# A hand-paced first pass becomes a table of single-engine pieces: block attention with two feed-forward layers

## The chip, the cores and the metric

The kernel runs on one core of one Trainium2 chip. The metric is device time in microseconds (us) from launch to end. A profiled execution adds a trace, in which the span runs from the first to the last instruction.

## The reference, cut to what matters

```python
# attention inside chunks of 64 tokens: q, k, v are (4, 8, 576, 64)
scores = q_c @ k_c^T / 8;  attn = exp(scores - max) / (sum + 1e-9);  x = attn @ v_c
# x becomes (2304 tokens, 512)
h = x @ w_in1;  g = s * relu(h)**2 + b;          x = g @ w_out1     # 512 -> 2048 -> 512
h = x @ w_in2;  g = h * tanh(log1p(exp(h)));     out = g @ w_out2   # 512 -> 2048 -> 512
```

All data are float32, and the weights arrive as 64-bit words.

## The kernel before, in words

**Tiles.** The 2304 tokens are 18 attention tiles of 128 tokens, gathered in five blocks of 512, 256, 512, 512 and 512 tokens (tiles 0 to 3, 4 and 5, 6 to 9, 10 to 13, 14 to 17). Each feed-forward layer has 16 columns of 128 hidden units (`f`), worked in four groups of four. So there are eight groups, each with 20 steps (five blocks times four `f`). A step is one `mm_in` (12 matmuls into a bank `hp`), the elementwise work that ends in two operands `ghi` and `glo`, and one `mm_out` (12 matmuls into the four sum banks `acc0` to `acc3`). Matmul operands are split in a high and a low part, so that each product takes three matmuls. Before a weight can be used it is loaded (`load_w`, 512 KB) and decoded: one ACT operation, four on DVE, a copy on ACT (`decode_hi`), and a subtraction on DVE (`decode_lo`). A group has eight such parts.

**Attention of a tile.** TensorE transposes k (`k_pe`, 4 matmuls), ACT copies it out in two halves into a block-diagonal key buffer `kbd` (`k_out`). The same for q (`q_pe`, `q_out`). Then 16 score matmuls (`s_pe`), max and subtraction on DVE (`s_max`), exp on ACT (`s_exp`), sum, reciprocal and scaling (`s_sum`), a transpose of the result (`p_pe`, `p_out`), 32 small matmuls with v (`x_pe`), and a split into high and low part (`x_out`: ACT, then DVE).

**Order.** Each engine works through its instructions in the order in which the program gives them. The first pass (attention, group 0 of layer 1) is ordered by hand under `manual_schedule`. First all early loads are issued (`LOADS`); the v loads of tiles 0 to 3 (`V0` to `V3`, four DMAs each) go through ACT's own DMA queue, all others through SP's. Then the string `START` runs tiles 0 to 3 and the decoding of the first two weight parts. Its `w3` and the like are idle matmuls on zeros. After it, a loop of 17 steps puts one step of group 0 together with pieces of four later tiles: x of tile step+1, p of step+2, scores of step+3, k and q of step+4. One weight part or two are decoded per step where `DECODE` says so. In this loop the attention has two PSUM banks (`ps_t`); `ps_at` gives the first four tiles seven banks in turn. Key buffers are four for the first four tiles, and one (`kbd[0]`) afterwards. After `no_sync_barrier` the last three steps of group 0 and groups 1 to 7 follow, put in order by the framework's scheduler, with the `mm_out` of a step two steps behind its `mm_in`.

Of the kernel before, what the change touches and what calls it, by code (L numbers as in the profile page):

```python
# [15 lines left out]
P = 128  # L16
# [16 lines left out]
def chunk_attention_moe_moe_kernel(  # L33
# [44 lines left out]
    ps_t = ctx.enter_context(tc.tile_pool(name="ps_t", bufs=2, space=bass.MemoryType.PSUM))  # L78
# [31 lines left out]
    def decode_w(l, f, part):  # L110
        decode_a(l, f, part)
        decode_b(l, f, part)

    def decode_a(l, f, part):
        decode_a1(l, f, part)
        decode_a2(l, f, part)

    def decode_a1(l, f, part):
# [18 lines left out]
    def decode_a2(l, f, part):  # L137
# [11 lines left out]
    def decode_b(l, f, part):  # L149
        decode_hi(l, f, part)  # L150
        decode_lo(l, f, part)

    def decode_hi(l, f, part):
# [20 lines left out]
    kbd = {}  # L174
# [53 lines left out]
    def transposes(i, src):  # L228
        p = ps_at(i, [P, KD, P])
# [4 lines left out]
    def k_pe(i):  # L234
        at[i]["kp"] = transposes(i, at[i]["k"].rearrange("p h d -> p (h d)"))

    def k_out(i, alt=False):
        kb = kbd[i if i < NS else 0]
# [5 lines left out]
        at[i]["kb"] = kb

    def q_pe(i):
        at[i]["qp"] = transposes(i, at[i]["q"].rearrange("p h d -> p (h d)"))

    def q_out(i, alt=False):
        at[i]["qt"] = sb_at(i, "qt").rearrange("p (a s) -> p a s", a=KD)  # L250
        eng = nc.vector.tensor_copy if alt else nc.scalar.copy
        eng(out=at[i]["qt"], in_=at[i].pop("qp"))
        if NS <= i and i + 2 < NTILE:
            load_qk(i + 2, "k")
            load_qk(i + 2, "q")

    def s_pe(i):
        t = at[i]
        t["sp"] = ps_at(i, [P, H, CH])
# [50 lines left out]
    def x_out(i, alt=False):  # L310
        xp = at.pop(i)["xp"]
        b, o = home[i]
        hi, lo = xhi[b][:, :, o:o + P], xlo[b][:, :, o:o + P]
        nc.scalar.activation(out=hi, in_=xp, func=AF.Copy)
        nc.vector.tensor_tensor(out=lo, in0=xp, in1=hi.bitcast(F32), op=ALU.subtract)  # L315
        if NS <= i and i + 3 < NTILE:
            load_v(i + 3)


    def mm_in(l, f, b, spare):  # L320

        n = sizes[b]
        pool, tag = (ps_t, "t") if spare and f % 2 else (ps_h, "h")
# [25 lines left out]
    def ew_b(l, r, n):  # L349
        hi = sb.tile([P, TB], F32R, tag="ghi", bufs=3, name="ghi")[:, :n]  # L350
        lo = sb.tile([P, TB], F32R, tag="glo", bufs=3, name="glo")[:, :n]
        if l == 1:
            nc.scalar.activation(out=r, in_=r, func=AF.Identity, bias=b_sb[:, 0:1])  # L353
        nc.scalar.activation(out=hi, in_=r, func=AF.Copy)  # L354
        nc.vector.tensor_tensor(out=lo, in0=r, in1=hi.bitcast(F32), op=ALU.subtract)  # L355
        return hi, lo
# [17 lines left out]

    def add_up(l, grp, b, acc):

        t0, n = blocks[b]
        for m, a in enumerate(acc):
            w = n if l == 1 else DM
            y = ysum[b][:, m * w:(m + 1) * w]  # L380
            if grp == 0:
                if m % 2:
                    nc.vector.tensor_copy(out=y, in_=a[:, :w])
                else:
                    nc.scalar.copy(out=y, in_=a[:, :w])
# [18 lines left out]

    pend = []
    accs = {}

    def out_half(h):
        l, grp, b, f, g = pend[0]
        if h == 0 and f % FG == 0:  # L410
            accs[l, b] = [
                ps_acc.tile([P, TB], F32, tag=f"acc{m}", name=f"acc{m}")
                for m in range(KD if l == 1 else sizes[b] // P)
            ]
        mm_out(l, f, g, accs[l, b], sizes[b], h)
        if h == 1:
            pend.pop(0)
            if f % FG == FG - 1:
                add_up(l, grp % NG, b, accs.pop((l, b)))

    first, second = chunk_parts(0), chunk_parts(1)
    DECODE = {0: first[2:4], 1: first[4:6], 2: first[6:7], 3: first[7:8]}
    DECODE.update(zip((7, 9, 10, 11, 13, 14, 15, 16), ([z] for z in second)))
    with tc.manual_schedule():
        nc.scalar.preload_act_table_set("exp_and_others")
        for w in LOADS.split():
            i = int(w[1:])
            if w[0] == "W":
                load_w(*first[i])
            elif w[0] in "vV":  # L430
                load_v(i, nc.scalar if w[0] == "V" else nc.sync)
            elif w[0] == "s":
                nc.sync.dma_start(out=s_sb, in_=s_in.partition_broadcast(P))
                nc.sync.dma_start(out=b_sb, in_=b_in.partition_broadcast(P))
            else:
                load_qk(i, w[0])
        x_tiles(0)
# [3 lines left out]
        warm = ps_t.tile([P, TB], F32, tag="t", name="warm")  # L441

        def warm_up(n):
            for _ in range(n):
                nc.tensor.matmul(out=warm[:, :P], lhsT=zero, rhs=zero)

        kbd[0] = atp.tile([P, KD, 2, P], F32, name="kbd")
# [131 lines left out]
```

## Time and profile before

| | us |
|---|---|
| median of 3 runs (range) | 922.19 (921.17 to 923.06) |
| profiled execution, its own time | 922.06 |
| its span | 920.3 |
| PE, DVE, ACT busy | 880.0, 480.9, 368.7 |

PE is TensorE's matmuls, PEld its weight loads, DVE VectorE, ACT ScalarE, POOL GpSimd; SPq and ACTq are DMA issues from those queues. PEclk is the granted TensorE clock as a share of 2.4 GHz (0.5 is 1.2 GHz). Matmul ends are modelled, and a row's duration runs a little into the next row; the distance between starts is the safer number. The windows view lists, for each stretch, its length, each engine's busy us with its instructions in brackets, PEclk, the DMA engines' busy share and GB/s. The lines view gives busy us in total, mean ns of one, and the idle time before.

### The profile page before, as it was taken

The page shows a single profiled execution, that of the slowest core. Times are in us where ns is not written, and L with a number is a line of the kernel's source. Part 1 is how long each engine was busy: PE and PEld are TensorE (multiplying, and loading weights), DVE is VectorE, ACT ScalarE, POOL GpSimd, SP SyncE. Part 2 cuts the span into 40 slices and gives each one's busy share as a digit, 9 for nine tenths or more (in the row PEclk, how much of TensorE's full clock was granted, in tenths as well). Part 3 has the DMA queues.
Part 4 walks back from the last instruction along what each step waited for, and adds up shares of the span by engine and source line. Part 5 has one row for each costly group of instructions (what it writes and reads, how often), then busy time and mean ns, then how long its engine had stood idle before and what let it go on. Part 6 is the DMA issues. An engine that isn't in the chain of part 4 may idle for free.

```text
span 920.3 us, 12036 instructions
## 1 busy us (share of the span) xinstructions
PE 880.0 (96%) x4878; PEld 735.8 (80%) x4878; DVE 480.9 (52%) x851; ACT 368.7 (40%) x643; POOL 33.9 (4%) x33
## 2 busy tenths in 40 slices
PE   4878889999999999999999999999999999999998
PEld 4656777778888888888988888888888888888886
DVE  1767667768833694359635971166225932222223
ACT  1555556656543463334544542233222322222221
POOL 1100000000000000000212220000000000000000
PEclk7978999999999999999999999999999999999999
DMA  9524463205000410023001400041003200001012
GB/s 251 149 47 115 121 162 98 46 1 160 24 1 1 124 59 1 1 69 115 1 1 37 125 22 1 5 133 46 0 1 93 90 1 1 0 1 46 24 46 91
DMA packets 81526, 53.20 MB, mean 58 GB/s; under 512 B 58688, under 2 KB 75072, under 8 KB 81472
## 3 DMA queue, kind: packets, MB, share of 16 engines
q1 hardware_dynamic: 77120, 51.39, 19.1%
q10 hardware_dynamic: 4352, 1.05, 0.5%
q8 instruction: 38, 0.62, 0.3%
q14 instruction: 16, 0.13, 0.0%
HBM read 47.71 MB, written 4.72 MB: 57 GB/s over the span
## 4 chain that ended last, share of the span: by engine, by line
PE 82%; DVE 9%; ACT 5%; DMA 2%; issue 1%; POOL 0%; DVEq 0%; ACTq 0%; POOLq 0%
PE hp L331 41%; PE acc L368 39%; DMA v<-in_v_dram 2%; DVE wdec L144 1%; DVE wdec L140 1%; ACT e L281 1%; ACT kbd L243 1%; ACT w L157 1%; DVE sm L286 1%; DVE e L275 1%; DVE xlo L315 1%; DVE mx L274 1%; DVE e L290 1%; DVE w L162 1%; DVE wdec L132 1%
## 5 line engine op out<-in xcount | busy, mean ns | idle before, releaser
L331 PE MATMUL hp<-xhi,w 128*128 128x512 f32 (+1 forms) x1280 | 373.1, 373 | 2.6 <-ACT w L157 1.7
L331 PEld LDWEIGHTS hp<-xhi,w 128*128 128x128 f32 x1280 | 233.3, 190 | 47.1 <-issue 2.7
L331 PE MATMUL hp<-xlo,w 128*128 128x512 f32 (+1 forms) x640 | 237.6, 371 | 0.1
L355 DVE TENSOR_TENSOR glo<-r,ghi 128x512 fp32r<-128x512 f32 (+1 forms) x160 | 104.9, 656 | 215.3 <-ACT ghi L354 214.9
L368 PE MATMUL acc<-ghi,w 128*128 128x512 f32 (+1 forms) x640 | 164.8, 375 | 2.5 <-DVE w L162 1.9
L368 PE MATMUL acc<-w,ghi 128*128 128x512 f32 x576 | 159.6, 390 | 0.0
L346 ACT ACTIVATE r<-hp 128x512 f32<-128x512 f32 (+1 forms) x80 | 44.4, 555 | 255.1 <-PE hp L331 255.1
L331 PEld LDWEIGHTS hp<-xlo,w 128*128 128x128 f32 x640 | 121.6, 190 | 21.6 <-DVE xlo L315 0.8
L368 PEld LDWEIGHTS acc<-ghi,w 128*128 128x128 f32 x640 | 113.7, 190 | 22.1 <-DVE w L162 2.2
L368 PEld LDWEIGHTS acc<-w,ghi 128*128 128x128 f32 x576 | 106.9, 188 | 21.3
L387 DVE TENSOR_TENSOR ysum<-acc,ysum 128x512 f32<-128x512 f32 (+1 forms) x114 | 71.8, 655 | 59.5 <-PE acc L368 59.5
L341 ACT ACTIVATE r<-hp 128x512 f32<-128x512 f32 (+1 forms) x80 | 44.1, 551 | 132.1 <-PE hp L331 132.0
L354 ACT ACTIVATE ghi<-r 128x512 fp32r<-128x512 f32 (+1 forms) x160 | 94.1, 588 | 4.5
L368 PE MATMUL acc<-glo,w 128*128 128x512 f32 (+1 forms) x320 | 94.1, 370 | 0.0
L368 PE MATMUL acc<-w,glo 128*128 128x512 f32 x288 | 93.9, 389 | 0.0
L342 DVE SCALAR_TENSOR_TENSOR r<-r,s_sb 128x512 f32<-128x512 f32 (+1 forms) x80 | 56.4, 705 | 67.3 <-ACT r L341 67.2
L353 ACT ACTIVATE r<-r,b_sb 128x512 f32<-128x512 f32 (+1 forms) x80 | 54.6, 682 | 51.2 <-DVE r L342 51.0
L368 PEld LDWEIGHTS acc<-glo,w 128*128 128x128 f32 x320 | 58.4, 189 | 10.3
L368 PEld LDWEIGHTS acc<-w,glo 128*128 128x128 f32 x288 | 54.1, 188 | 11.3
L157 ACT ACTIVATE w<-wdec 128x512 fp32r<-128x512 f32 x64 | 40.3, 630 | 54.4 <-DVE wdec L144 54.0
L162 DVE TENSOR_TENSOR w<-wdec,w 128x512 fp32r<-128x512 f32 x64 | 44.9, 703 | 2.9 <-ACT w L157 2.0
L140 DVE SCALAR_TENSOR_TENSOR wdec<-wraw,wdec 128x512 uint32<-128x512 uint32 x64 | 44.0, 693 | 0.6
(302 smaller groups left out, 494.7 us busy)
## 6 DMA issues: line engine op xcount, KB each, us to landing
wraw<-in_moe_w_in_dram SPq DMA_DIRECT2D x32, 512.0 KB, 3.9
wraw<-in_moe_w_out_dram SPq DMA_DIRECT2D x32, 512.0 KB, 3.5
out_dram<-ysum SPq DMA_DIRECT2D x18, 256.0 KB, 2.0
k<-in_k_dram SPq DMA_DIRECT2D x16, 256.0 KB, 2.9
v<-in_v_dram SPq DMA_DIRECT2D x56, 64.0 KB, 3.3
q<-in_q_dram SPq DMA_DIRECT2D x12, 256.0 KB, 2.9
v<-in_v_dram ACTq DMA_DIRECT2D x16, 64.0 KB, 4.1
k<-in_q_dram SPq DMA_DIRECT2D x4, 256.0 KB, 4.8
```

The costliest lines, as they stand in the source:

```text
L140: nc.vector.scalar_tensor_tensor(out=u, in0=t[:, :, 1], scalar=0xC0000000, in1=u, op0=ALU.bitwise_and, op1=ALU.bitwise_or,)
L157: nc.scalar.activation(out=w[:, 0], in_=a, func=AF.Copy)
L162: nc.vector.tensor_tensor(out=lo, in0=a, in1=hi.bitcast(F32), op=ALU.subtract)
L331: nc.tensor.matmul(out=hp, lhsT=w[:, sl], rhs=r[b][:, a, :], start=(a == 0 and p == 0), stop=(a == KD - 1 and p == 2),)
L341: nc.scalar.activation(out=r, in_=hp, func=AF.Relu)
L342: nc.vector.scalar_tensor_tensor(out=r, in0=r, scalar=s_sb[:, 0:1], in1=r, op0=ALU.mult, op1=ALU.mult)
L346: nc.scalar.activation(out=r, in_=hp, func=AF.Mish)
L353: nc.scalar.activation(out=r, in_=r, func=AF.Identity, bias=b_sb[:, 0:1])
L354: nc.scalar.activation(out=hi, in_=r, func=AF.Copy)
L355: nc.vector.tensor_tensor(out=lo, in0=r, in1=hi.bitcast(F32), op=ALU.subtract)
L368: nc.tensor.matmul(out=acc[m][:, :n] if l == 1 else acc[m], lhsT=w[wi][:, sl] if l == 1 else g[gi][:, sl], rhs=g[gi] if l == 1 else w[wi], ...
L387: nc.vector.tensor_tensor(out=y, in0=a[:, :w], in1=y, op=ALU.add)
```

## The change

`LOADS`, the loop of 17 steps and `DECODE` go. The whole first pass, with all 20 steps of group 0 and all its loads, becomes one table `START` of 600 pieces, each of which runs on one engine or issues one load. A piece may name its PSUM bank (`@0` to `@3` are the sum banks, `@4` and `@5` the two banks that attention had before) or its key buffer (`.0` to `.2`, three instead of four and one). The letters: `dk dq dv` loads of a tile, `W` load of a weight part, `K Q S T X` the matmuls of k, q, scores, transposed p and x; `k q m e n z t x y` what ACT and DVE do after them (`n` sum and reciprocal, `z` scaling, `x` high and `y` low part); `a c d h l` the steps of decoding; `I J` and `O P` the halves of `mm_in` and `mm_out`; `r u v g o` the elementwise work; `E` the first sums, each copied out alone; `w` idle matmuls. `I5` is step 5.

Tiles start in the order 3, 2, 4, 0, 7, 1, 5, 6, 8 and so on. Only tile 0's v goes through ACT's queue. All scalings run on DVE (three of the first four were on GpSimd), and all copies of k, q and p on ACT (`alt` is gone). Of group 1's eight weight parts five are decoded in the table and three (`parts[13:]`) at the start of group 1. Groups 1 to 7 are unchanged, but now start with no `mm_out` pending.

```diff
-LOADS = "k0 q0 V0 k1 q1 V1 k2 q2 V2 W0 k3 q3 V3 W1 k4 q4 W2 W3 s0 k5 q5 v4 W4 W5 v5 W6 W7 v6"
+
 START = (
...
+    "dk3 dq3 dv0 dv3 K3@4 dk2 dq2 k3.0 w3 Q3@5 dk4 q3 dq4 w9 S3@0 W0 dk0 sb m3 w3 K2@1 dv2 k2.1 w3 Q2@2 e3 w3 "
+    "K4@3 q2 n3 dk7 k4.2 S2@4 W5 z3 Q4@5 dv4 m2 a0 T3@0 q4 t3 w3 K0@1 c0 e2 S4@2 k0.0 W2 d0 X3@3 dk1 dq1 K7@5 n2 "
+    "h0 x3 dq7 m4 a5 W4 k7.1 dk5 y3 e4 dq5 c5 a2 dq0 z2 dv1 d5 w24 K1@4 T2@0 k1.2 Q1@1 n4 h5 w3 Q7@2 q1 c2 W3 t2 "
+    "S1@5 dq9 q7 z4 dv5 d2 X2@3 T4@4 l5 x2 K5@1 h2 S7@0 m1 k5.2 W1 Q0@2 dk6 y2 a4 Q5@5 dk8 q0 m7 q5 dq8 w4 S0@1 "
+    "e1 l2 t4 dv7 S5@3 e7 m0 a3 X4@2 n1 e0 Q9@5 W7 x4 n0 dv6 q9 y4 w15 K6@0 z0 k6.1 m5 w3 T0@4 dk9 K8@1 t0 dq10 "
+    "z1 Q8@5 k8.0 X0@2 dk10 n7 e5 dq13 T1@0 q8 c3 x0 W6 S8@3 t1 n5 X1@4 d3 K9@1 x1 y0 h3 dk13 z7 k9.2 w3 Q10@5 z5 "
+    "dq6 T7@0 q10 K10@2 l3 t7 T5@1 y1 dk14 k10.0 X7@5 l0 W10 a1 c4 I2 W12 a7 dv8 x7 c1 t5 I0 d4 X5@0 d1 W9 h4 J0 "
+    "W11 x5 dv9 c7 h1 J2 y5 r0 l1 S9@4 d7 r2 W13 a6 I3 W14 u2 W15 h7 Q6@2 W8 l4 v2 J3 dq14 l7 q6 g2 y7 I1 a10 u0 "
+    "a12 o2 S6@1 v0 m8 r3 J1 g0 m6 e8 I4 K13@0 o0 J4 e6 dk11 u3 k13.2 Q13@2 K14@5 n6 dq11 r1 v3 m9 dk12 I5 q13 g3 "
+    "J5 k14.1 u1 O0 o3 v1 z6 e9 P0 r4 n8 n9 T6@4 g1 I6 t6 z8 J6 o1 X6@5 z9 r5 u4 O1 u5 x6 dv10 c6 v4 v5 T8@4 y6 "
+    "P1 t8 d6 X8@5 g4 c10 h6 S13@4 x8 dv13 o4 l6 I7 r6 y8 a9 O2 u6 m13 v6 Q11@5 P2 q11 dq12 d10 e13 T9@4 g5 O3 "
+    "n13 t9 h10 o5 X9@5 E0.0 E0.1 S10@4 z13 x9 dv12 l10 P3 y9 a11 m10 Q12@5 g6 I8 E0.2 dq15 E0.3 q12 e10 J7 o6 "
+    "c12 O4 r7 n10 J8 u7 I9 z10 v7 r8 c9 P4 u8 J9 g7 d9 v8 O5 o7 I10 h9 c11 r9 l9 P5 u9 T10@4 a8 O6 d12 g8 v9 "
+    "T13@5 P6 t10 o8 t13 J10 d11 g9 h12 X13@4 o9 r10 h11 X10@5 l12 x13 dv14 u10 O7 x10 y13 I11 v10 E1.1 E1.0 y10 "
+    "dv11 K11@4 l11 P7 k11.2 c8 K12@5 J11 E1.2 E1.3 g10 d8 dk17 k12.0 S11@4 dk16 r11 o10 S12@5 h8 m11 O8 m12 e11 "
+    "Q14@4 P8 q14 dq17 n11 e12 S14@5 u11 n12 O9 v11 m14 g11 K17@4 P9 k17.2 dk15 o11 z11 e14 Q17@5 O10 z12 q17 "
+    "dq16 n14 T11@4 T12@5 l8 t11 P10 z14 t12 T14@4 X11@5 t14 O11 x11 dv17 y11 X14@4 E2.0 E2.1 X12@5 x14 dv16 P11 "
+    "y14 x12 y12 S17@4 E2.2 E2.3 dv15 I12 m17 I13 e17 K15@5 n17 J13 k15.0 z17 Q15@4 r13 K16@5 J12 q15 u13 k16.1 "
+    "S15@4 v13 r12 I14 g13 m15 I15 u12 e15 o13 J14 v12 n15 g12 Q16@5 r14 T17@4 z15 J15 q16 o12 t17 u14 S16@5 r15 "
+    "v14 O12 u15 g14 m16 T15@4 v15 P12 t15 o14 e16 X15@5 g15 n16 O13 x15 o15 z16 X17@4 y15 P13 x17 y17 T16@5 O14 "
+    "t16 X16@4 P14 x16 y16 O15 I16 E3.0 E3.1 P15 J16 E3.2 E3.3 I17 r16 u16 I18 v16 J17 g16 o16 J18 r17 u17 I19 "
+    "r18 v17 u18 O16 g17 v18 J19 o17 g18 P16 o18 r19 u19 O17 v19 g19 P17 o19 O18 P18 O19 E4.0 E4.1 P19 E4.2 E4.3"
 )
...
-    ps_t = ctx.enter_context(tc.tile_pool(name="ps_t", bufs=2, space=bass.MemoryType.PSUM))
+    ps_t = ctx.enter_context(tc.tile_pool(name="ps_t", bufs=1, space=bass.MemoryType.PSUM))
...
+    def ps_at(b, shape):
+
+        if b < KD:
+            return ps_acc.tile(shape, F32, tag=f"acc{b}", name="pa")
+        return ps_t.tile(shape, F32, tag=f"t{b - KD}", name="pt_")
...
-    def k_out(i, alt=False):
-        kb = kbd[i if i < NS else 0]
+    def k_out(i, n):
+        at[i]["kb"] = kb = kbd[n]
...
-            eng = nc.vector.tensor_copy if alt and j else nc.scalar.copy
-            eng(out=kb[sl, :, :, sl], in_=kp[sl])
...
+            nc.scalar.copy(out=kb[sl, :, :, sl], in_=kp[sl])
...
-        eng = nc.gpsimd if i < NS and not alt else nc.vector
-        eng.tensor_tensor(out=e, in0=e, in1=sm.to_broadcast([P, H, CH]), op=ALU.mult)
...
+    def s_norm(i):
+        e = at[i]["e"]
+        nc.vector.tensor_tensor(out=e, in0=e, in1=at[i].pop("sm").to_broadcast([P, H, CH]), op=ALU.mult)
...
+        elif name == "dv":
+            load_v(i, nc.sync if i else nc.scalar)
...
+        rest = parts[13:] if grp == 1 else []
+        for step in range(NB * FG):
             b, f = step // FG, f0 + step % FG
+            for z in rest[2 * step:2 * step + 2]:
+                decode_w(*z)
```

## Rows read from the trace of the kernel before

**Rows 1.** The page, part 2: the span in 40 slices of 23 us.
```profile
PE   4878889999999999999999999999999999999998
PEclk7978999999999999999999999999999999999999
```

**Rows 2.** Windows view: three stretches of the first pass, its end, two later groups.
```profile
0.00:42.10 42.10, 26.34 (x294) 23.45 (x295) 17.98 (x36) 15.37 (x28) 7.39 (x13) 0.84 0.83 219
42.10:126.48 84.38, 69.83 (x594) 57.29 (x594) 55.19 (x103) 45.07 (x83) 0.00 (x0) 0.88 0.40 100
126.48:202.89 76.41, 70.90 (x627) 56.14 (x625) 54.46 (x101) 45.30 (x82) 0.00 (x0) 1.00 0.27 67
202.89:221.00 18.11, 18.11 (x79) 14.67 (x80) 13.29 (x23) 9.46 (x16) 0.00 (x0) 1.00 0.46 136
221.00:319.66 98.66, 98.66 (x482) 83.58 (x481) 58.02 (x102) 48.38 (x82) 0.00 (x0) 1.00 0.13 41
319.66:418.32 98.66, 98.66 (x482) 83.58 (x481) 57.65 (x102) 44.15 (x75) 0.00 (x0) 1.00 0.14 43
```

**Rows 3.** Timeline of the start: start us, us, engine, line, operation, idle before.
```profile
0.76 16.24 ACTq L224 DMA_DIRECT2D v<-in_v_dram  x16
4.63 1.92 PE L231 MATMUL pa<-ident,k 128*128 128x128 f32 x8
17.10 0.58 ACT L243 COPY kbd<-pa 64x512 f32<-64x512 f32 x1 [15.09 <-DMA v<-in_v_dram]
18.55 1.98 PE L263 MATMUL pa<-kbd,v 128*64 128x128 f32 x16 [10.83 <-DVE kbd L243]
20.57 0.69 DVE L274 TENSOR_REDUCE mx<-pa 128x8 f32<-128x512 f32 x1 [1.20 <-PE pa L263]
42.10 1.01 PE L331 MATMUL hp<-xhi,w 128*128 128x512 f32 x2 [1.67 <-ACT w L157]
```

**Rows 4.** Waits view of PE, 42 to 126.5 us: total us, times, longest.
```profile
PE pt__519 L263 <- ACT qt L252: 3.7, 1, 3.7
PE acc L368 <- DVE w L162: 1.9, 1, 1.9
```

**Rows 5.** Timeline of PE: one piece of each kind at full clock.
```profile
142.83 0.60 PE L231 MATMUL pt__1432<-ident,q 128*128 128x128 f32 x4
143.36 1.15 PE L308 MATMUL pt__1445<-e,v 64*64 64x64 f32 x32
176.77 1.09 PE L263 MATMUL pt__1799<-kbd,qt 128*64 128x128 f32 x16
210.12 0.62 PE L331 MATMUL hp<-xhi,w 128*128 128x512 f32 x2
212.84 1.98 PE L368 MATMUL acc<-ghi,w 128*128 128x512 f32 x8
```

**Rows 6.** Lines view by shape, DVE and ACT, 0 to 221 us.
```profile
L144 DVE SCALAR_TENSOR_TENSOR wdec<-wraw,wdec 128x512 uint32<-128x512 uint32 x18 | 12.5, 692 | 0.6
L132 DVE TENSOR_SCALAR wdec<-wdec 128x512 uint32<-128x512 uint32 x18 | 7.7, 427 | 0.6
L288 DVE RECIPROCAL sm<-sm 128x8 f32<-128x8 f32 x18 | 3.7, 203 | 0.6
L342 DVE SCALAR_TENSOR_TENSOR r<-r,s_sb 128x512 f32<-128x512 f32 x15 | 11.2, 747 | 11.3 <-ACT r L341 11.3
L281 ACT ACTIVATE e<-e 128x512 f32<-128x512 f32 x18 | 11.4, 631 | 6.2 <-DVE e L275 6.2
L353 ACT ACTIVATE r<-r,b_sb 128x512 f32<-128x512 f32 x15 | 10.9, 726 | 3.6 <-DVE r L342 3.5
```

**Rows 7.** DMA: rate of the first 35 us in 40 slices, and issues from SP.
```profile
GB/s 0 0 108 283 287 280 278 289 287 287 304 387 315 288 288 341 379 290 286 230 164 131 364 354 327 50 171 289 249 126 86 280 301 205 324 277 220 378 417 320
1.85 0.91 SPq L211 DMA_DIRECT2D k<-in_k_dram  x1
76.85 2.58 SPq L224 DMA_DIRECT2D v<-in_v_dram  x4
```

More of the change, by code (lines that the diff above doesn't have):

```diff
@@ L1 @@
+import re
 from contextlib import ExitStack
@@ L126, in decode_a1, with decode_c @@
             nc.vector.tensor_scalar(
-                out=u, in0=t[:, :, 1], scalar1=0x7FFFFFFF, scalar2=None, op0=ALU.bitwise_and
+                out=a.bitcast(U32), in0=t[:, :, 1], scalar1=0x7FFFFFFF, scalar2=None, op0=ALU.bitwise_and
             )
+    def decode_c(l, f, part):
+        t, a = raw[l, f, part]
+        u = a.bitcast(U32)
         nc.vector.tensor_scalar(
@@ L135, in decode_a1, with decode_d @@
         )
-    def decode_a2(l, f, part):
+    def decode_d(l, f, part):
         t, a = raw[l, f, part]
@@ L147, in decode_a2, with decode_h @@
         )
[L149 to L153, printed above, removed]
+    def decode_h(l, f, part):
         a = raw[l, f, part][1]
@@ L157, in decode_hi, with decode_l @@
         nc.scalar.activation(out=w[:, 0], in_=a, func=AF.Copy)
-    def decode_lo(l, f, part):
+    def decode_l(l, f, part):
         hi, lo = wt[l, f, part]
@@ L162, in decode_lo, with decode_w @@
         nc.vector.tensor_tensor(out=lo, in0=a, in1=hi.bitcast(F32), op=ALU.subtract)
+    def decode_w(*z):
+        for step in (decode_a, decode_c, decode_d, decode_h, decode_l):
+            step(*z)
     def runs(t0, n):
@@ L227, in load_v, with transposes @@
                     )
-    def transposes(i, src):
-        p = ps_at(i, [P, KD, P])
+    def transposes(b, src):
+        p = ps_at(b, [P, KD, P])
         for a in range(KD):
@@ L232, in transposes, with k_pe @@
         return p
[L234 to L238 removed]
+    def k_pe(i, b):
+        at[i]["kp"] = transposes(b, at[i]["k"].rearrange("p h d -> p (h d)"))
+    def k_out(i, n):
+        at[i]["kb"] = kb = kbd[n]
         kp = at[i].pop("kp").rearrange("p a (c s) -> p a c s", c=2)
@@ L241, in k_out, with q_pe, q_out, s_pe @@
             sl = slice(j * CH, (j + 1) * CH)
-            eng = nc.vector.tensor_copy if alt and j else nc.scalar.copy
-            eng(out=kb[sl, :, :, sl], in_=kp[sl])
[L244 to L249, printed above, removed]
-        at[i]["qt"] = sb_at(i, "qt").rearrange("p (a s) -> p a s", a=KD)
[L251 to L257, printed above, removed]
+            nc.scalar.copy(out=kb[sl, :, :, sl], in_=kp[sl])
+    def q_pe(i, b):
+        at[i]["qp"] = transposes(b, at[i]["q"].rearrange("p h d -> p (h d)"))
+    def q_out(i):
+        at[i]["qt"] = sb_at(i, "qt").rearrange("p (a s) -> p a s", a=KD)
+        nc.scalar.copy(out=at[i]["qt"], in_=at[i].pop("qp"))
+    def s_pe(i, b):
         t = at[i]
-        t["sp"] = ps_at(i, [P, H, CH])
+        t["sp"] = ps_at(b, [P, H, CH])
         for a in range(KD):
@@ L347, in ew_a, with ew_u, ew_v, ew_g @@
         return r
-    def ew_b(l, r, n):
+    def ew_u(r):
+        nc.vector.scalar_tensor_tensor(
+            out=r, in0=r, scalar=s_sb[:, 0:1], in1=r, op0=ALU.mult, op1=ALU.mult
+        )
+    def ew_v(r):
+        nc.scalar.activation(out=r, in_=r, func=AF.Identity, bias=b_sb[:, 0:1])
+    def ew_g(r, n):
         hi = sb.tile([P, TB], F32R, tag="ghi", bufs=3, name="ghi")[:, :n]
+        nc.scalar.activation(out=hi, in_=r, func=AF.Copy)
+        return hi
+    def ew_o(r, hi, n):
         lo = sb.tile([P, TB], F32R, tag="glo", bufs=3, name="glo")[:, :n]
+        nc.vector.tensor_tensor(out=lo, in0=r, in1=hi.bitcast(F32), op=ALU.subtract)
+        return lo
+    def ew(l, hp, n):
+        r = ew_r(l, hp, n)
         if l == 1:
[L353 to L356, printed above, removed]
+            ew_u(r)
+            ew_v(r)
+        hi = ew_g(r, n)
+        return hi, ew_o(r, hi, n)
     def mm_out(l, f, g, acc, n, h):
@@ L373, in mm_out, with first_sum @@
             )
+    def first_sum(b, m, a, eng):
+        y_tile(b)
+        n = sizes[b]
+        eng(out=ysum[b][:, m * n:(m + 1) * n], in_=a[:, :n])
     def add_up(l, grp, b, acc):
@@ L381, in add_up @@
             if grp == 0:
[L382 to L385, printed above, removed]
+                (nc.vector.tensor_copy if m % 2 else nc.scalar.copy)(out=y, in_=a[:, :w])
                 continue
@@ L403, in chunk_parts @@
         return sorted(z, key=lambda z: (z[1] + z[2], z[2]))
[L405 to L419, printed above, removed]
@@ L421, in chunk_attention_moe_moe_kernel, with new_accs, pieces @@
-    first, second = chunk_parts(0), chunk_parts(1)
-    DECODE = {0: first[2:4], 1: first[4:6], 2: first[6:7], 3: first[7:8]}
-    DECODE.update(zip((7, 9, 10, 11, 13, 14, 15, 16), ([z] for z in second)))
+    parts = chunk_parts(0) + chunk_parts(1)
+    ff = {}
+    first_acc = {}
+    def new_accs(l, b):
+        return [
+            ps_acc.tile([P, TB], F32, tag=f"acc{m}", name=f"acc{m}")
+            for m in range(KD if l == 1 else sizes[b] // P)
+        ]
+    def pieces(name, i, m, bank):
+        b, f = divmod(i, FG)
+        n = sizes[b] if b < NB else 0
+        if name in ("dk", "dq"):
+            load_qk(i, name[1])
+        elif name == "dv":
+            load_v(i, nc.sync if i else nc.scalar)
+        elif name == "sb":
+            nc.sync.dma_start(out=s_sb, in_=s_in.partition_broadcast(P))
+            nc.sync.dma_start(out=b_sb, in_=b_in.partition_broadcast(P))
+        elif name in "KQSTX":
+            dict(K=k_pe, Q=q_pe, S=s_pe, T=p_pe, X=x_pe)[name](i, bank)
+        elif name == "k":
+            k_out(i, m)
+        elif name in "qmenztxy":
+            dict(q=q_out, m=s_max, e=s_exp, n=s_sum, z=s_norm, t=p_out, x=x_hi, y=x_lo)[name](i)
+        elif name in "Wacdhl":
+            dict(W=load_w, a=decode_a, c=decode_c, d=decode_d, h=decode_h, l=decode_l)[name](*parts[i])
+        elif name == "w":
+            for _ in range(i):
+                nc.tensor.matmul(out=warm[:, :P], lhsT=zero, rhs=zero)
+        elif name == "I":
+            ff[i] = {}
+            ff[i]["h"], ff[i]["half"] = mm_in(1, f, b, False)
+            ff[i]["half"](0)
+        elif name == "J":
+            ff[i]["half"](1)
+        elif name == "r":
+            ff[i]["r"] = ew_r(1, ff[i]["h"], n)
+        elif name == "u":
+            ew_u(ff[i]["r"])
+        elif name == "v":
+            ew_v(ff[i]["r"])
+        elif name == "g":
+            ff[i]["g"] = ew_g(ff[i]["r"], n)
+        elif name == "o":
+            ff[i]["o"] = ew_o(ff[i]["r"], ff[i]["g"], n)
+        elif name in "OP":
+            if name == "O" and f == 0:
+                first_acc[b] = new_accs(1, b)
+            mm_out(1, f, (ff[i]["g"], ff[i]["o"]), first_acc[b], n, "OP".index(name))
+        elif name == "E":
+            first_sum(i, m, first_acc[i][m], nc.vector.tensor_copy if m % 2 else nc.scalar.copy)
+        else:
+            raise ValueError(name)
@@ L424, in chunk_attention_moe_moe_kernel @@
     with tc.manual_schedule():
         nc.scalar.preload_act_table_set("exp_and_others")
[L426 to L436, printed above, removed]
@@ L440, in chunk_attention_moe_moe_kernel @@
         make_identity(nc, ident)
[L441 to L447, printed above, removed]
+        warm = ps_h.tile([P, TB], F32, tag="h", name="warm")
         room = sb.tile([P, 2, KD, 2, P], F32, tag="ysum3", name="kbd12")
-        kbd[1], kbd[2] = room[:, 0], room[:, 1]
-        kbd[3] = sb.tile([P, KD, 2, P], F32, tag="ysum2", name="kbd3")
@@ L451, in chunk_attention_moe_moe_kernel @@
-        for kb in kbd.values():
+        kbd = [atp.tile([P, KD, 2, P], F32, name="kbd"), room[:, 0], room[:, 1]]
+        for kb in kbd:
             nc.gpsimd.memset(kb, 0.0)
-        by_name = dict(w=warm_up, K=k_pe, k=k_out, Q=q_pe, q=q_out, S=s_pe, m=s_max, e=s_exp, n=s_sum,
-                       T=p_pe, t=p_out, X=x_pe, x=x_out,
-                       A=lambda i: decode_a(*first[i]), B=lambda i: decode_b(*first[i]))
         for w in START.split():
-            by_name[w[0]](int(w[1]), *[True] * (w[2:] == "*"))
@@ L524, in chunk_attention_moe_moe_kernel, with do_out @@
-        for z in late:
-            decode_lo(*z)
-    tc.no_sync_barrier()
-    for grp in range(2 * NG):
+            name, i, m, bank = re.fullmatch(r"([a-zA-Z]+)(\d*)(?:\.(\d))?(?:@(\d))?", w).groups()
+            pieces(name, int(i or 0), int(m or 0), int(bank or 0))
+    tc.no_sync_barrier()
+    pend = []
+    accs = {}
+    def do_out():
+        l, grp, b, f, g = pend.pop(0)
+        if f % FG == 0:
+            accs[l, b] = new_accs(l, b)
+        for h in range(2):
+            mm_out(l, f, g, accs[l, b], sizes[b], h)
+        if f % FG == FG - 1:
+            add_up(l, grp % NG, b, accs.pop((l, b)))
@@ L529, in chunk_attention_moe_moe_kernel @@
+    for grp in range(1, 2 * NG):
         l, f0 = chunks[grp * FG]
-        to_load, to_decode = (chunk_parts(grp + 1), chunk_parts(grp + 1)) if grp else ([], [])
-        for step in range(0 if grp else NTILE - 1, NB * FG):
+        to_load, to_decode = chunk_parts(grp + 1), chunk_parts(grp + 1)
+        rest = parts[13:] if grp == 1 else []
+        for step in range(NB * FG):
             b, f = step // FG, f0 + step % FG
+            for z in rest[2 * step:2 * step + 2]:
+                decode_w(*z)
```

140 lines of the change are left out of this document (28 added, 112 removed).

## The prediction

> **What bounds the kernel now.** I read the page first [rows 1]. From its tenth slice on, PE is full at the full clock; all that can be won lies in the first 220 us, and the granted clock is low only there. The windows put borders to it [rows 2]. A later group of 20 steps takes 98.66 us with PE busy for all of it; two in a row agree to the hundredth. So from 221.0 us on, where PE begins group 1, the kernel is bound by PE, and 699.3 of the 920.3 us lie there.
>
> The first pass needs far less PE time than the 221.0 us it takes. A q transpose is 0.60, the scores 1.09, the x matmuls 1.15 us [rows 5]; neighbouring rows overlap by some 0.07, as the q row that starts at 142.83 and the x row at 143.36 show. A tile is three transposes at 0.59, 1.03 and 1.08, which is 3.9 us, and 18 tiles are 70. A half step is 2.72 us (from 210.12 to 212.84 for 12 matmuls), half of that in block 1, and a group is 98. Before 221.0 us PE does all attention and group 0 but two `mm_out`: 70 + 98 - 5.4 = 163 us. So 58 us are lost, and the stretches of [rows 2] say where.
>
> In 0 to 42.1 us, four tiles are 15.5 us of work: 26.6 lost. In 42.1 to 126.5 PE does steps 0 to 7, the `mm_out` of steps 0 to 6, and 8 k, 8 q, 8 scores, 6 p, 6 x: 59 us of work, 25 lost. Of these, 14.5 are idle time (84.4 less 69.8 busy) and the rest is the clock, granted at 0.88. In 126.5 to 202.9 it is 69 us of work, 7 lost; to 221.0 almost nothing.
>
> The reasons differ. At the start, k was transposed at 4.63 us, but ACT copied it out only at 17.10, since it stood in its own queue of 16 v issues for 16.24 us; the first scores came at 18.55 [rows 3]. Later PE waits for whatever the hand order put in its way: 3.7 us for `qt`, which ACT copies late, 1.9 for a decoded weight [rows 4]. No other engine is full: DVE is busy for 55 of 84 us, ACT for 45.
>
> **The change, part by part.** *ACT's queue.* Twelve of 16 v issues move to SP. On ACT they took 16.24 us together [rows 3], so four take about 4. The first k copy can start at some 5 us, the first scores at 7 to 8 and the first max at 9, where it was at 20.57. SP pays instead: 2.58 us for four v issues [rows 7], 7.7 for twelve.
>
> *The loads.* In front of `dk10`, the last load that the PE pieces before `I2` need, the table has 20 k and q, 8 v and 7 W. The first k and q loads ran at some 283 GB/s [rows 7], 0.93 us for 256 KB (an issue that waits for room took 0.91), and 28 of them are 26 us. W runs at 340 or more, 1.5 us each, 10.5 in all. By the DMA engines that is 37 us. By SP's issues, if nothing overlaps, it is 20 x 0.93 + 7 x 2.58 + 10.5 + 1 = 48. A wait of SP for a free buffer would come on top. Landing included, I take 47, with 40 and 52 as the ends.
>
> *DVE and ACT.* A full-width DVE operation is 0.69 us (0.75 with `s`, 0.43 for the two short ones of decoding, 0.20 for a reciprocal), one on ACT 0.58 to 0.73 [rows 6]. By these a tile costs DVE 3.9 us, a weight part 3.0, a step 1.4; three scalings more than before are 2.1, two half copies fewer give 1.4 back. The 13 parts, 18 tiles, 20 steps and the sums make 141 us on DVE and 121 on ACT. Neither reaches PE's 168 + 10 for idle matmuls, so over the whole pass PE has to be the bound; but not in each part of it.
>
> *The table by stages.* I counted pieces up to four marks and multiplied by these prices.
> Up to `I2`: PE 11 K, 10 Q, 8 S, 7 T, 6 X, which is 31 us (and 76 idle matmuls, up to 10); DVE 7 m, 7 n, 7 z, 5 y, 5 c, 4 d, 4 l, 39 us. DVE can't start before 9, so `I2` comes no earlier than 48; loads say 47 to 50. With the gaps of the first tiles I take 53 (48 to 60).
> `I2` to `I8`: PE 40.3, DVE 40.2, ACT 31. Two full engines that hand each other their work won't both stay full. The best stretch of attention before reached 69 of 76.4, or 0.90, with DVE at 54 [rows 2], and lost its time to the hand order, not to DVE. I take 0.90: 44.8 us.
> `I8` to `I12`: PE 43.4, DVE 36.4. At 0.94, 46.2 us.
> `I12` to the end: PE 53.0, DVE 25.5; at 0.98, 54.1 us.
> PE ends the table at 53 + 44.8 + 46.2 + 54.1 = 198.1. All 20 `mm_out` are in it, two more than in the 221.0.
>
> *The banks.* From `O0` on attention has the two banks that it had before. In front of it, sum banks spread the first tiles; what this saves is in the stage up to `I2`, which isn't bound by banks. Three key buffers let a k copy go ahead of the scores of the tile before; nothing in the stage sums hangs on it, so I give it neither gain nor cost.
>
> *The border.* Group 1 starts with nothing pending. Its first three `mm_in`, 8.2 us, run without a partner, and the three remaining weight parts are decoded in front of its elementwise work. One part is a chain of 0.67 + 0.42 + 0.43 + 0.69 + 0.69 + 0.63 + 0.69 = 4.2 us over ACT and DVE, two are about 7.5 if one follows the other, and the step's own chain to `ghi` takes 2.8 more. That is 10.3 against 8.2 of cover, and the next step repeats a part of it: 2.5 us, between 0 (the scheduler finds room) and 6. The group itself has 5.4 us less to do.
>
> **Sum.** 920.3 - 221.0 + 198.1 - 5.4 + 2.5 = 894.5 us of span. The profiled execution was 922.06, 1.8 over its span and 0.1 from the median, so 896.3; I say 896, a gain of 26 us.
>
> **Rivals.** *The table doesn't fit the chip.* An order made for other durations and landing times makes each engine wait for its neighbour, as the hand order did between 42.1 and 126.5 us. For it: DVE and PE are equally full up to `I8`, and all queues are in order. Against it: a piece is now one engine's work, so a copy no longer sits behind a decoding of which it needs nothing. If PE gets 0.78 from `I2` to `I12`, the two stretches take 107 instead of 91, and the time is 912 (908 to 920).
> *The table is denser than I grant.* `I2` at 48 and 0.97 everywhere: 48 + 41.5 + 44.7 + 54.1 = 188, no loss at the border: 884. Gaps on DVE and late loads speak against it.
> *The clock falls: slower.* PE alternates between short pieces and waits, and in the 84 us in which it did so before the clock was granted at 0.88. The first 16 score matmuls took 1.98 us where warm ones take 1.09 [rows 3, 5], so what is run cold costs double. If PE in the table waits often and briefly, the 83.7 us from `I2` to `I12` stretch by their inverse: with a mean grant of 0.70 by 36 us, to 932. The point from which it decides is 0.76, where they cost the 26 us. The 76 idle matmuls all stand before `I2` and don't help there. Against it: from 126.5 us on the loop ran at the full clock although PE was idle for 5.5 of 76.4 us [rows 2], and the table has more work in each stretch.
> The Trainium skill, "TensorE: Matmul & The Clock Gate", section "A second HAM failure mode: psum-queue depth-cycling", says that a kernel which cycles through PSUM banks leaves TensorE idle for short moments so often that its clock swings between its two levels. By that rule the table, with two banks in turn from `O0` on, would lose its gain here; the full clock of the loop after 126.5 us, on the same two banks [rows 2], speaks against it.
> *Nothing comes of it.* The win at the start is given back by SP and the border: 922. PE's idle time before is real and the start on ACT is sure to go, so this needs two rivals at once.
>
> **Chances.** The forecast, 884 to 908: 0.62. Denser, under 884: 0.08. The ill-fitting table, 908 to 920: 0.20. About as before: 0.04. Slower by the clock: 0.06. The measurement tells 0.2%, 1.8 us, from no change. So faster 0.90, same 0.04, slower 0.06. The range from 881 to 916 leaves out some 0.05 below and 0.15 above; the forecast's own range is 884 to 908.
>
> **What the profile after would show.** The first scores by 8 us, the first `hp` matmuls of `I2` at about 53, not 42. The DMA engines busy without a break to about 50 us. From `I2` to `I8` PE and DVE both at nine tenths. The last `acc` matmul of group 0 at about 198, then a gap of some 2 us on PE and a group of 98.66 - 5.4 us; groups 2 to 7 as before. The forecast is wrong if `I2` comes after 60, if PE waits on one producer at each tile, if the granted clock stays under 0.9 after `I2`, or if SP waits for buffers before 50 us.

## The result and the profile after

The changed kernel takes 890.2 us (median of 4 runs, 889.4 to 891.1). In the same session the kernel before took 921.7 (921.1 to 923.1). The ratio is 0.9656, with a 95% interval of 0.964 to 0.9673: 31.5 us faster. The forecast was 896, with a range of 881 to 916. The profiled execution took 889.39 us, of which 887.6 are span. PE is now busy for 99% of it.

The page after, part 2 (the span in 40 slices, of 22.2 us each) and the first line of part 4, the chain that ended last:

```profile
PE   8989999999999999999999999999999999999997
...
DVE  4878875459736943488348922473227722222122
...
PEclk9999999999999999999999999999999999999999
DMA  8996131040004200140004100230003100001012
...
PE 97%; ACT 1%; DMA 1%; DVE 0%; issue 0%; DVEq 0%; ACTq 0%
```

PE has no slice under eight tenths except the last, and no slice of a low clock; before it had both [rows 1]. The eights at the start flatter it, since idle matmuls count as busy. The windows view, cut where PE reaches `I2` (55.89), `I8` (97.15), `I12` (140.34) and group 1 (193.63); the last row is group 1:

```profile
0.00:55.89 55.89, 47.84 (x585) 44.40 (x585) 35.21 (x70) 34.84 (x61) 3.38 (x9) 1.00 0.91 221
55.89:97.15 41.26, 40.97 (x371) 33.85 (x367) 36.53 (x69) 28.84 (x55) 0.00 (x0) 1.00 0.66 178
97.15:140.34 43.19, 43.19 (x418) 36.51 (x416) 33.54 (x63) 26.82 (x49) 0.00 (x0) 1.00 0.28 64
140.34:193.63 53.29, 53.29 (x350) 43.33 (x349) 24.17 (x40) 25.63 (x43) 0.00 (x0) 1.00 0.22 72
193.63:286.90 93.27, 93.27 (x457) 79.05 (x456) 65.93 (x121) 49.16 (x87) 0.00 (x0) 1.00 0.10 33
```

From 55.89 us on PE is full at the granted clock 1.00. In the second row it is full while DVE is busy for 36.53 of 41.26 us. The waits view of PE from 56 to 194 us has a single row:

```profile
PE hp L344 <- ACT r L354: 0.3, 1, 0.3
```

The rows that answer to [rows 3], from the timeline of the start (start, duration, engine, line, operation, idle before):

```profile
0.76 2.95 ACTq L238 DMA_DIRECT2D v<-in_v_dram  x4
...
3.89 1.09 PE L246 MATMUL pt__101<-ident,k 128*128 128x128 f32 x4 [3.89 <-DMA k<-in_k_dram]
...
5.07 1.19 ACT L257 COPY kbd<-pt__101 64x512 f32<-64x512 f32 x2 [3.06 <-PE pt__101 L246]
...
9.84 1.09 PE L272 MATMUL pa<-kbd,v 128*64 128x128 f32 x16
...
10.99 0.69 DVE L283 TENSOR_REDUCE mx<-pa 128x8 f32<-128x512 f32 x1 [9.99 <-PE pa L272]
```

ACT's queue is free at 3.7 us, where it was taken until 17, and k is copied out as soon as it is transposed. The first max comes 9.6 us earlier. Further down the timeline stand the largest block of idle matmuls, the last two waits before `I2`, the start of `I2`, and the border to group 1:

```profile
20.67 5.52 PE L466 MATMUL warm<-zero 128*128 128x128 f32 x48
...
50.90 0.63 PE L246 MATMUL pa<-ident,k 128*128 128x128 f32 x4 [1.86 <-DMA k<-in_k_dram]
...
53.79 0.65 PE L246 MATMUL pa<-ident,k 128*128 128x128 f32 x4 [0.72 <-DMA k<-in_k_dram]
...
55.89 0.72 PE L344 MATMUL hp<-xhi,w 128*128 128x512 f32 x2
...
193.63 0.62 PE L344 MATMUL hp<-xhi,w 128*128 128x512 f32 x2
...
204.84 1.52 PE L395 MATMUL acc<-ghi,w 128*128 128x512 f32 x6
```

**Where the time came from.** By the prediction's prices PE has 31.2 us of useful work before `I2`, so 24.7 of the 55.9 us are lost there. After `I2` it has 40.3 + 43.4 + 53.0 = 136.7 us of work and takes 137.7: 1 us is lost. Group 1 to the end takes 694.0 us, where 699.3 - 5.4 = 693.9 are needed. Before, 26.6 us were lost up to 42.1 us and 32 after it. So nearly all of the loss behind the start is gone, and the start, though it now does twice the work (31 us against 15.5), still loses about what it lost.

### The profile page after: what moved, and what is told of

It is laid out like the page before. It is cut to its first block, busy times and chain, and to the rows that moved or that the text cites. A ratio compares the mean times of both kernels' runs of the same rounds, so it can differ in the third digit from the quotient of the medians.

```text
span 887.6 us, 12275 instructions
## 1 busy us (share of the span) xinstructions
PE 874.8 (99%) x4976; PEld 737.9 (83%) x4976; DVE 477.7 (54%) x852; ACT 370.9 (42%) x645; POOL 30.0 (3%) x29
## 4 chain that ended last, share of the span: by engine, by line
PE 97%; ACT 1%; DMA 1%; DVE 0%; issue 0%; DVEq 0%; ACTq 0%
PE hp L344 45%; PE acc L395 45%; PE warm L466 2%; DMA k<-in_k_dram 1%; PE pa L272 1%; ACT kbd L257 1%; PE pa L246 1%; PE pa L318 0%; DVE ysum L416 0%; ACT e L290 0%; ACT v L264 0%; PE pt__383 L272 0%; PE pt__195 L272 0%; PE pt__101 L246 0%; PE pt__2009 L318 0%
## 5 line engine op out<-in xcount | busy, mean ns | idle before, releaser
L344 PE MATMUL hp<-xhi,w 128*128 128x512 f32 (+1 forms) x1280 | 368.6, 369 | 0.3 <-ACT r L354 0.3
L395 PE MATMUL acc<-ghi,w 128*128 128x512 f32 (+1 forms) x640 | 162.8, 372 | 0.0
```

Source lines behind the costliest of these rows:

```text
L344: nc.tensor.matmul(out=hp, lhsT=w[:, sl], rhs=r[b][:, a, :], start=(a == 0 and p == 0), stop=(a == KD - 1 and p == 2),)
L395: nc.tensor.matmul(out=acc[m][:, :n] if l == 1 else acc[m], lhsT=w[wi][:, sl] if l == 1 else g[gi][:, sl], rhs=g[gi] if l == 1 else w[wi], ...
```

## The experiments

Each kernel ran next to the kernel before on the same chip. Costs are taken from the ratios, 0.001 being 0.92 us, against the changed kernel's 0.9656. The interval of each ratio is 1.3 to 2.7 us to either side, and that of the changed kernel 1.5, so a difference under some 2 to 3 us isn't told apart.

**Early v loads on ACT's queue.** The changed kernel, with the v of tiles 0 to 3 issued first on ACT.

```diff
-            load_v(i, nc.sync if i else nc.scalar)
+            if i >= NS:
+                load_v(i)
...
+        for i in range(NS):
+            load_v(i, nc.scalar)
```

> The changed kernel, with the v loads of tiles 0 to 3 all issued first on ACT's queue again (16 issues), and no longer from SP at their places. If the win at the start comes from ACT being free at 4 us, the first scores come at 18 us instead of 9.8, everything behind them moves, and the time rises by 8 to 10 us, to about 899. If the stage up to I2 is bound by the loads that SP issues, SP is freed of 9 us of v issues, I2 stays near 56 us and the time stays within 2 us of 890.

Measured: 897.9 us, ratio 0.975 (0.9735 to 0.9764), 8.7 us more. Its timeline:

```profile
0.77 16.04 ACTq L238 DMA_DIRECT2D v<-in_v_dram  x16
...
16.91 1.18 ACT L257 COPY kbd<-pt__111 64x512 f32<-64x512 f32 x2 [14.90 <-issue]
...
18.85 1.98 PE L272 MATMUL pa<-kbd,v 128*64 128x128 f32 x16 [9.72 <-ACT v L264]
...
64.50 0.73 PE L344 MATMUL hp<-xhi,w 128*128 128x512 f32 x2
```

The first scores come 9 us later and `I2` 8.6 us later. Nothing of it is made good afterwards.

**The same move alone, in the kernel before.**

```diff
-LOADS = "k0 q0 V0 k1 q1 V1 k2 q2 V2 W0 k3 q3 V3 W1 ..."
+LOADS = "k0 q0 V0 k1 q1 v1 k2 q2 v2 W0 k3 q3 v3 W1 ..."
```

> The kernel before, with one edit: v of tiles 1 to 3 is loaded by SP, behind q of the same tile; v of tile 0 stays on ACT. If ACT's queue was the whole loss at the start, first scores at 8 us instead of 18.5 and the first hp matmuls 10 us earlier: 912. If the loads bound the start anyway, the first hp matmuls stay at 40 to 44 us and the time is 919 to 924.

Measured: 913.2 us, ratio 0.9917 (0.9902 to 0.9932), 7.6 us less than before. Its timeline has the first scores at 7.29 us and the first `hp` matmuls at 36.17, where they were at 42.10 [rows 3]:

```profile
7.29 1.09 PE L263 MATMUL pa<-kbd,v 128*64 128x128 f32 x16
...
36.17 1.00 PE L331 MATMUL hp<-xhi,w 128*128 128x512 f32 x2 [1.67 <-ACT w L157]
```

ACT's queue cost 7.6 us in the kernel before and 8.7 in the changed one; it is a quarter of the gain and needs no table.

**No idle matmuls.** The `w` pieces issue nothing.

```diff
-            for _ in range(i):
+            for _ in range(0):
```

> The changed kernel without its idle matmuls (76 pieces, all before I2). If they only fill waits: 890, within 1 us. If they hold the clock: granted clock near 0.5 in the first 40 us, I2 2 to 8 us later and the first steps cold, 893 to 900. If they stand in the way of work that is ready (they fill PE for some 17 us before I2), I2 comes 2 to 5 us earlier: 885 to 888.

Measured: 888.8 us, ratio 0.9653 (0.9638 to 0.9668): no difference. Its windows up to `I2`:

```profile
0.00:25.00 25.00, 14.50 (x120) 11.89 (x121) 13.22 (x27) 14.13 (x23) 3.37 (x9) 0.95 0.92 220
25.00:55.16 30.16, 23.69 (x314) 20.11 (x312) 22.30 (x44) 20.82 (x38) 0.00 (x0) 0.87 0.89 222
```

PE's two longest waits there:

```profile
PE pt__298 L246 <- DMA k<-in_k_dram: 5.0, 1, 5.0
PE pt__101 L246 <- DMA k<-in_k_dram: 3.7, 1, 3.7
```

The granted clock falls to 0.87 between 25 and 55 us, and `I2` still begins at 55.16. PE doesn't bound that stage. The 5.0 us wait for a k load stands where the table has 24 idle matmuls.

**Pieces glued together again.** Neighbouring pieces of a tile, a weight part or a step are issued as one, as the functions before did. PE and SP keep their order. The cut names the pairs by their letters; in the table they are brought together at each place where they stand.

```diff
-n3 ... z3      x3 ... y3       # attention: sum with scaling, high with low part
-a0 ... c0      d0 ... h0       # decoding: ACT with DVE, DVE with ACT
-r0 ... u0      v0 ... g0 o0    # elementwise: ACT with DVE, the rest in one
+n3 z3          x3 y3
+a0 c0          d0 h0
+r0 u0          v0 g0 o0
```

> The changed kernel with the same table, but the pieces glued together again as the functions before had them: sum with scaling (n z), high with low part of x (x y), first two and next two steps of a decoding (a c, d h), Relu with square (r u), and bias, high and low part of the elementwise work (v g o). The order on PE and SP is the same. If splitting into single-engine pieces is what lets PE run without a wait after I2, PE waits return there: 5 to 15 us, 895 to 905. If the order of the matmuls and loads is what counts, the time stays within 2 us of 890.

Measured, all three kinds: 906.9 us, ratio 0.9847 (0.9828 to 0.9866), 17.6 us more (16.7 by the two times alone, the figure in the expectations below).

Attention alone:

> The changed kernel with only the attention pieces glued: sum with scaling (n z) and high with low part of x (x y). If the 16.7 us that all gluing cost come from attention's chains on DVE, most of them return here: 8 us or more. If they come from one of the other two groups, under 3 us.

Measured: 889.9 us, ratio 0.9665 (0.9641 to 0.969): no difference.

Decoding alone:

> The changed kernel with only the decoding glued: a with c, and d with h. ACT then stands at the copy h until DVE has done d, which is how the hand order made PE wait for qt. If this is the cost of gluing, 8 us or more; else under 3 us.

Measured: 895.3 us, ratio 0.9718 (0.9697 to 0.974), 5.7 us more.

Elementwise work alone:

> The changed kernel with only the elementwise work glued: r with u, and v with g and o. If this is the cost of gluing, 8 us or more; else under 3 us. If the three groups add up, the three times exceed 890 by 16.7 us in sum.

Measured: 891.1 us, ratio 0.9677 (0.9653 to 0.9701), 1.9 us, not told from nothing. The three alone come to 8.4 us, where together they cost 17.6.

Decoding and elementwise work glued, attention not:

> The changed kernel with decoding and elementwise work glued, attention split as it is. Glued alone they cost 5 and 1 us, attention 0, all three 16.7. If the costs grow because two glued chains hold each other up on ACT and DVE, this costs 12 us or more (902 and up). If attention's glue is what is needed for the rest, 6 to 8 us (896 to 898).

Measured: 906.6 us, ratio 0.9852 (0.9824 to 0.9881), 18.1 us more, as with all three glued. So the pair makes the cost. The longest waits of ACT and of PE in this kernel, from 56 to 200 us:

```profile
ACT w L174 <- DVE wdec L165: 13.6, 8, 2.9
...
PE hp L345 <- ACT r L355: 4.4, 1, 4.4
```

Its timeline behind `I2`:

```profile
65.03 0.63 ACT L174 ACTIVATE w<-wdec 128x512 fp32r<-128x512 f32 x1 [2.92 <-DVE wdec L165]
...
65.57 0.58 ACT L355 ACTIVATE r<-hp 128x512 f32<-128x512 f32 x1
...
66.19 0.75 DVE L361 SCALAR_TENSOR_TENSOR r<-r,s_sb 128x512 f32<-128x512 f32 x1 [1.24 <-ACT r L355]
...
75.68 0.63 ACT L291 ACTIVATE e<-e 128x512 f32<-128x512 f32 x1 [1.96 <-DVE e L285]
...
77.40 0.60 ACT L355 ACTIVATE r<-hp 128x512 f32<-128x512 f32 x1
...
78.05 0.79 PE L345 MATMUL hp<-xhi,w 128*128 128x256 f32 x2 [4.40 <-ACT r L355]
```

Its windows row from `I2` on:

```profile
55.42:97.00 41.58, 37.18 (x301) 30.94 (x298) 32.37 (x61) 24.39 (x44) 0.00 (x0) 0.92 0.63 172
```

The rows at 65 us are the pattern. ACT's copy of a decoded weight (`w`) is issued right behind the DVE operation that it needs, so ACT stands still for 2.9 us; the next step's `r` is queued behind it; DVE then waits 1.2 us for that `r`. At 75.68 us it is DVE that is late: ACT waits 2.0 us for an `e`, the `r` that frees a bank for `hp` stands behind it, and PE waits 4.4 us. That the waits at 65 us are what made DVE late ten microseconds on is argued from the order of the pieces, not shown row by row. In the changed kernel, where other work lies between `d` and `h`, ACT's waits for `wdec` in these 144 us come to 1.1 us, and those for `e` to 5.0 instead of 11.2. In some 41.5 us behind `I2` PE gets through 301 matmul records instead of 371.

**Three banks instead of six before `O0`.** Attention uses one sum bank and the two that it had before. Some pieces move by a few places, since a bank must have been read before it is taken again.

```diff
-"... K3@4 ... Q3@5 ... S3@0 ... K2@1 ... Q2@2 ... K4@3 ..."
+"... K3@3 ... Q3@4 ... S3@5 ... K2@3 ... Q2@4 ... K4@5 ..."
```

> The changed kernel in which the attention pieces in front of O0 have three banks (the fourth sum bank and the two of ps_t) in place of six; each engine's order is the same. By the prediction banks don't bound the stage up to I2: within 2 us of 890. If early sum banks are the source of what freeing ACT and splitting leave unexplained, some 7 us slower: 895 to 900.

Measured: 896.7 us, ratio 0.9737 (0.9713 to 0.9761), 7.5 us more. `I2` begins at 59.74. Below the wait for the first k load, PE's waits up to 60 us now name the ACT copies that empty a bank:

```profile
...
PE pt__440 L273 <- ACT kbd L258: 1.3, 1, 1.3
PE pt__383 L273 <- ACT pt L309: 1.0, 1, 1.0
PE pt__732 L319 <- ACT kbd L258: 0.8, 1, 0.8
PE pt__710 L247 <- ACT qt L265: 0.7, 1, 0.7
PE pt__700 L247 <- ACT kbd L258: 0.7, 1, 0.7
```

Two banks alone weren't tried.

**All three undone.** v on ACT, all pieces glued, three banks: what is left of the change is its order, its bookkeeping of keys, and its copies on ACT and scaling on DVE. It isn't the kernel before in another order: there the first four tiles had seven banks in turn, here all early tiles share three.

> The changed kernel with three parts undone at once: the early v on ACT's queue, all pieces glued, three banks in front of O0. The order of matmuls and loads stays that of the table. If these three are the whole gain, it is back at 918 to 922 (890 + 7.7 + 16.7 + 6 = 920). If the table's order of tiles and matmuls has a worth of its own, it stays at 905 to 914.

Measured: 932.6 us, ratio 1.0129 (1.0105 to 1.0154): 12 us slower than the kernel before, and 43.6 above the changed one, where the three add up to 8.7 + 17.6 + 7.5 = 33.8. Its window up to `I2`:

```profile
0.00:81.75 81.75, 58.30 (x585) 52.32 (x585) 37.40 (x73) 36.01 (x62) 3.38 (x9) 0.83 0.65 163
```

`I2` comes at 81.75, 26 us later, though v on ACT alone moves it by 8.6 and three banks alone by 3.9. Here the clock was granted at 0.83 and the DMA engines were busy for 0.65: the loads wait too. Why the parts grow by some 10 us together isn't settled.

**What sets `I2`.** Without idle matmuls, and the v of tile 2 issued by ACT instead of SP:

```diff
-            load_v(i, nc.sync if i else nc.scalar)
+            load_v(i, nc.scalar if i in (0, 2) else nc.sync)
...
-... dk4 q3 dq4 ... K2@1 dv2 k2.1 ...
+... dk4 q3 dv2 dq4 ... K2@1 k2.1 ...
```

> The changed kernel without idle matmuls, and with v of tile 2 issued by ACT right behind q3, where ACT waits 4.6 us for k of tile 2. SP then gets to all later loads 2.6 us earlier. If the loads bound the stage up to I2, I2 comes 1.5 to 2.5 us earlier and the time is 886 to 887. If DVE bounds it, no change: 889.

Measured: 890.4 us, ratio 0.9673 (0.9652 to 0.9695): no difference; `I2` at 55.86. The same, with one weight part and the v of tile 4 issued later:

```diff
-... Q4@5 dv4 m2 a0 ... W2 d0 X3@3 dk1 dq1 K7@5 ... dq7 m4 ...
+... Q4@5 m2 a0 ... d0 X3@3 dk1 dq1 W2 K7@5 ... dq7 dv4 m4 ...
```

> The same, and the load of a second-layer weight part (W2) and of v of tile 4 moved behind k and q of tile 1, which PE waited for in front of K1. If the order of loads bounds the stage, K1 starts 2 to 4 us earlier and the time is 884 to 887; if DVE bounds it, the same as the run before it.

Measured: 888.6 us, ratio 0.9663 (0.9639 to 0.9686): no difference; `I2` at 55.09. The long wait for the k of tile 1 is gone from its timeline; a later one, of 3 us, is now the largest behind the first load:

```profile
41.74 1.09 PE L247 MATMUL pa<-ident,k 128*128 128x128 f32 x4 [2.98 <-DMA k<-in_k_dram]
```

The two runs before have a wait of 3.1 and 3.4 us at the same place (42.0 and 42.1 us), there put down to DVE, so it isn't new. The windows row of this last run up to 55.89 us has the rate of the changed kernel:

```profile
0.00:55.89 55.89, 40.80 (x436) 33.94 (x436) 35.70 (x71) 35.42 (x62) 3.38 (x9) 0.88 0.90 222
```

With three orders of loads the DMA engines are 0.89 to 0.91 busy and move 217 to 222 GB/s, and `I2` comes at 55.1 to 55.9. That fits a stage bound by the rate of the DMA engines. But SP's queue is as full: up to 50 us it issues almost without a break, and `dk10` is issued at 49.0 us in the changed kernel, at 49.3 without idle matmuls, and at 48.6 and 48.2 in these two. Nor was SP relieved of the full 2.6 us of four v issues: in the first of the two it lost 1.8 us in a wait for a v load (waits view of SP, 7 to 10 us):

```profile
SPq L226 <- DMA v<-in_v_dram: 1.8, 1, 1.8
```

By the expectations, no change would speak for DVE as the bound. The trace of the changed kernel doesn't bear that out: DVE's 35.2 us of work behind a first max at 11.0, without a wait, would end at 46. No run moved fewer bytes or larger pieces before `I2`, so which of the DMA engines and SP's queue sets `I2` stays open.

## Why the prediction was right, and where its sizes were off

*The bound and the place of the gain.* Right: everything was won before group 1, and groups 2 to 7 take what they took. The sum came out 6.9 us too high (894.5 against 887.6 of span), from three terms.

*`I2` at 53: it came at 55.9, +2.9.* The loads' price was too low, and the gaps behind it too high. The chain that ends in `I2` has this row for `dk10`:

```profile
49.01 4.74 DMA k<-in_k_dram
```

It was issued at 49.0 and landed at 53.7, where I had 47 with the landing included; `I2` followed 2.2 us later, where I had left 6 for gaps. So the 2.9 are 6.7 too little for the loads, less 3.8 too much for the gaps; that the one made up for half of the other is luck. I took the 283 GB/s of the best slices [rows 7] for the k, q and v loads and 340 for W, and got 37 us by the engines. The mean over the whole start stood in [rows 2]: 219 GB/s at 0.83 busy. In front of `dk10` lie 28 loads of 256 KB and 7 of 512 KB, 11.0 MB; at the 221 GB/s of the window after, that is 50 us. The other way, by SP's issues, I had 48, and the issue came at 49.0; what that leaves out is the landing. No run tells which of the two ways sets it.

*SP waits for buffers before 50 us.* I had named this as a sign that the forecast is wrong. It came: SP waited 1.4 us for a q transpose between 36 and 41 us, and 0.5 us once more later. Without idle matmuls the first is 0.3 us, and the time is the same; the sign was too strict.

*The first scores by 8 us: 9.84.* The k copy came at 5.07 as predicted. Eighteen rows of idle matmuls stand right in front of the scores; without them the first scores come at 6.82. I had priced the 76 at 10 us in all; 24 of them take 5.52 us, 0.23 each, 17.5 in all. It cost nothing that can be told, as the run without them shows: there PE waits instead, for loads most of all.

*`I2` to the end at 145.1 us: 137.7, -7.4.* The forecast's 0.90, 0.94 and 0.98 of PE were 0.98, 1.00 and 0.99. The step that failed: "two full engines that hand each other their work won't both stay full". PE stayed full with DVE at 0.89. I took 0.90 from a loop of glued functions, and the glued kernels show what gluing costs in this order; what it cost in the loop itself wasn't tried. I had named this reason only as an argument against a rival; it should have set the term.

*The border, 2.5 us: 0.1.* The scheduler put 11.2 us of `mm_in` in front of the first `acc` of group 1 (193.63 to 204.84), more than the 10.3 us of decoding and elementwise work that I had set against 8.2 of cover. The lower end of my bound held.

*The banks, nothing: 7.5 us.* The step "the stage up to `I2`, which isn't bound by banks" was wrong. With three of six banks `I2` moves by 3.9 us, and more follows behind it. The sum didn't show it, because I priced the stage by loads with all six banks in place. (In the profiled execution of that run, the fastest of its four, group 1 starts 5.3 us late, 3.9 of them in front of `I2`.) The three key buffers, put at nothing too, weren't tried by themselves.

*A price misread.* A transpose is 0.60 us in [rows 5], and its row and the next start 0.53 apart, yet I took 0.59. At 0.53 the 18 tiles are some 67 us of PE work instead of 70. This shifts each figure of lost time by 1 to 2 us and no conclusion.

*ACT's queue.* Right in place and mechanism, from both kernels (8.7 and 7.6 us).

**The rivals.** The ill-fitting table didn't come: PE's share from `I2` to `I12` was 0.99, not 0.78. But it is near: glue two kinds of pieces again, and the same order loses 18 us. The denser table was right after `I2` and wrong before it. The clock didn't fall: it was granted at 1.00 in every window, and the idle matmuls, which did keep it up before `I2`, bought no time. What I weighed as a rule of the Trainium skill ("TensorE: Matmul & The Clock Gate", section "A second HAM failure mode: psum-queue depth-cycling") is reported there of one kernel, which cycles through PSUM banks and whose TensorE is idle for short moments between groups of matmuls, often enough that its clock swings. Here attention had two banks from `O0` (75.94 us) on, and PE waited for nothing in the 117.7 us from there to group 1, at a granted clock of 1.00, so cycling through banks did not bring the idle moments. With decoding and elementwise work glued the waits are there, and the granted clock from 55.4 to 97 us is 0.92, in the direction of that report and small. "Nothing comes of it" fell with the result.

**What makes the gain.** Taken back one at a time, freeing ACT's queue is worth 8.7 us, the single-engine pieces 17.6, the six banks 7.5. With the three undone, the table's order is slower than the kernel before by 12 us, so the order doesn't pay without them. What it would do with glued pieces and the seven banks that the first tiles had before wasn't tried.

## What to carry to other kernels

Where two chains of work share two engines that run in order (here decoding and elementwise work, on ACT and DVE), a function that issues both engines' parts back to back makes each chain stand in the other's way; gluing the decoding alone cost 6 us, the elementwise work alone nothing that could be told, both 18, so try such cuts together. An engine that heads a chain shouldn't issue its own DMAs first, and banks that stand unused early were worth 7.5 us here. Price a stretch of loads by the mean rate of a stretch, not by its best slices, and add the landing of the last one.

## What the runs showed of the hardware that was not expected

PE stayed full for 41 us beside a DVE that was busy 0.89 of the time and an ACT at 0.70, with a chain running through all three. The DMA engines, 0.89 to 0.91 busy, moved only some 220 GB/s of mixed k, q, v and weight loads, where single slices had shown 283 to 417 [rows 7]. An idle matmul of 128x128 in f32 shows as two rows and takes 0.23 us at full clock. A granted clock of 0.91 over the first 55 us, without idle matmuls, cost no time that could be measured.
